# Clamp and integer addition of ten weight blocks on GpSimd, with overlapped steps

## The chip, the cores and the metric

The kernel runs on one core of a Trainium2 chip. The core has five engines, each with its own instruction queue that is worked off strictly in order: TensorE (PE) multiplies matrices into PSUM, VectorE (DVE) and ScalarE (ACT) do elementwise work, GpSimd (POOL) does elementwise work and here also issues the stores of results, and SyncE (SP) issues almost all other transfers (DMA) and computes nothing. Engines wait for each other through semaphores. The metric is the device time of one execution in microseconds, the median of several runs.

## The reference

An attention block without softmax is followed by a token-mixing and a channel-mixing MLP, all in float32:

```python
kv  = einsum('bhsd,bhse->bhde', k, v)             # 8 batches, 8 heads, 576 tokens, 64 per head
out = einsum('bhsd,bhde->bhse', q, kv)
out = out / sqrt(mean(out*out, -1) + 1e-6) * g_norm
x   = out, heads side by side                     # 8 x 576 x 512
u   = x + (relu(x.T @ w_tok1) @ w_tok2).T         # token mixing, 576 -> 256 -> 576
y   = u + relu(u @ w_ch1) @ w_ch2                 # channel mixing, 512 -> 1536 -> 512
```

w_ch1 (512 x 1536) and w_ch2 (1536 x 512) are the channel weights, the subject of the change.

## The kernel before, in words

**Stages.** Batches are worked on in pairs. For each pair the attention makes k'v per head (PSUM tiles ps_kv), multiplies it with q (ps_o, and ps_r for the last 64 tokens), and normalises into tiles x; the token mixing multiplies x with w_tok1 (ps_h), applies ReLU into h, multiplies with w_tok2 and adds x (ps_u), which gives u. POOL stores u (out_dram, and u_rest for the last 64 tokens of each batch). The channel mixing starts at about 183 us and fills the rest, to 768 us. It splits both matrix products into seven smaller ones, two levels deep, with sums of weights and of activations made by DVE. Attention and token mixing of the four pairs, and the preparation of the weights, fill the first 183 us.

**Rounding of weights.** Weights arrive as pairs of 32-bit words and are prepared in blocks by `decode` (L177): ACT scales the raw words (`high` L181 and `low` L186, or L196 and L199 in `scale_leaves` for w_ch2), then DVE does three steps on the block: `clamp` (L202, a minimum and a maximum), `shift` (L206, three bits to the left) and `add` (L211, a custom instruction that adds the other raw word as a 32-bit integer in two 16-bit limbs). There are fourteen channel blocks, numbered 0 to 13 here: eight of w_ch1, 128 partitions x 768 elements, and six of w_ch2, 128 x 1024. `block` (L222) adds `fetch`, the load of the raw words into a tile `raw` (by SP). Four raw tiles exist, so the fetch of block n+4 has to wait until the add of block n has read its tile.

**Order.** It is written out by hand. `start`, `middle`, `steady` and `last` (L1380 onward) are lists of words that `play` (L1319) works through, calling for each word a function that issues instructions; every engine and every DMA queue keeps this program order (`keep`). `kv`, `e`, `a`, `q`, `g`, `t`, `m`, `r`, `i`, `d`, `s`, `p` are steps of the attention of the next pair (`p` is a multiply of x by 1/rms on POOL, L570; `s` the same on ACT, L557; `d` on DVE, L566), `h`, `hr`, `u`, `z` steps of the token mixing, `l`, `lq`, `lr` loads of k, v and q. `f5` is the fetch of channel block 5. A number such as `1` or `2` plays so many steps of `rounding`, the iterator that `stream` (L1306) makes of the channel blocks: 43 steps in all, of which 31 are played in `middle` and `steady` and the others in `last`. The words around the end of the second `steady` list are

```python
"u3 z6 d11 1", "u4 s10 t40 t41 m2 r2 1",
"u5 i2 d20 p21 1", "u6 1 f12 b20 b21", "u7 1", "a3 q30 g31 q31 g30", "u8 t30 t31 m3 r3 f13"]]
```

`x` words transpose finished tiles into the room of w_ch2 that no block has been decoded into yet, and `b` words store these (SP, blocks<-w_ch, L124 like all loads and stores); the decoding of the last blocks has to wait until that room is empty.

**Helpers.** Many operations are recorded at the line of a helper: L124 a DMA on any queue, L127 a sum of two tiles, L130 a ReLU, L133 a copy on ACT, L136 a matrix product.

Of the kernel before, what the change touches and what calls it, by code (L numbers as in the profile page):

```python
# [15 lines left out]
ALU = mybir.AluOpType  # L16
# [4 lines left out]
def kernel(  # L21
# [32 lines left out]
    nc = tc.nc  # L54
    P = 128
    B, S, DM = k.shape
# [7 lines left out]
    NC, NF, NTOK = DM // P, DCH // P, DTOK // P  # L64
# [8 lines left out]
    T = 2 * P  # L73
    assert B // 2 == 4
    EPS = 1e-6
    TOP = (2.0 - 2.0 ** -3 - 2.0 ** -23) * 2.0 ** -96

    def pool(name, bufs, side="left", stack=ctx, **kw):
# [27 lines left out]
    w_ch1 = w1p.tile([P, 4, 4, FQ], F32, name="w_ch1")  # L106
# [8 lines left out]
    def do(f, *a, **kw):  # L115
        return lambda: f(*a, **kw)
# [4 lines left out]
    keep = tc.keep_in_program_order  # L121

    def dma(o, i, engine=nc.sync):
        keep(engine.dma_start(o, i))  # L124
# [49 lines left out]
            q_rest[b] = qtp.tile([P, HP, HF], F32, name="qR", tag="qR", bufs=4)  # L174
            dma(q_rest[b], q[b].rearrange("(c p) s -> p c s", p=P)[..., LO:])

    def decode(dst, raw, flat, leaves=False):  # L177

        bits = dst.bitcast(U32)
        def high():  # L180
            keep(nc.scalar.activation(dst, raw()[..., 1].bitcast(F32), AF.Prelu,  # L181
                                      scale=2.0 ** -112, alpha=2.0 ** 32))

        def low():
            t = raw()[..., 0]
            keep(nc.scalar.activation(t, t, AF.Copy, scale=2.0 ** -29))  # L186

        def scale():
            high()
            low()  # L190

        def scale_leaves():
            of = raw().rearrange("p (g b l j) w -> p g l b j w", g=4, b=NC, l=2)
            to = lambda t, l: t.rearrange("p (g l b j) -> p g l b j", g=4, l=2, b=NC)[:, :, l]
            for l in range(2):
                keep(nc.scalar.activation(to(dst, l), of[:, :, l, ..., 1].bitcast(F32), AF.Prelu,  # L196
                                          scale=2.0 ** -112, alpha=2.0 ** 32))
            for l in range(2):
                keep(nc.scalar.activation(to(raw()[..., 1], l), of[:, :, l, ..., 0], AF.Copy, scale=2.0 ** -29))  # L199

        def clamp():
            keep(nc.vector.tensor_scalar(out=dst, in0=dst, scalar1=TOP, scalar2=-TOP * 2.0 ** 32,  # L202
                                         op0=ALU.min, op1=ALU.max))

        def shift():
            keep(nc.vector.tensor_scalar(out=bits, in0=bits, scalar1=3, scalar2=None,  # L206
                                         op0=ALU.logical_shift_left))

        def add():
            o = bits.bitcast(U16)  # L210
            keep(nc.vector._custom_dve(ADD32_U16LIMBS, out=o, in0=o, in1=flat().bitcast(U16)[..., 2 * leaves:][..., :2]))  # L211

        return scale_leaves if leaves else scale, clamp, shift, add, high, low

    def words(w):
        return w.bitcast(U32).rearrange("r (n w) -> r n w", w=2)
# [2 lines left out]

        return flat if len(dst.shape) == 2 else flat.rearrange("p (a n) -> p a n", a=dst.shape[1])  # L220

    def block(n, loads, dst, leaves=False):  # L222

        raw = []

        def fetch():
            raw.append(stage.tile([P, n, 2], U32, name="raw", tag="raw", bufs=4))
            for o, i in loads(raw[0]):
                dma(o, i)

        def turn():
            t = raw[0]
            return t if len(dst.shape) == 2 else t.rearrange("p (a n) w -> p a n w", a=dst.shape[1])

        return (fetch,) + decode(dst, turn, lambda: raw[0], leaves)

    def get_tok1(i):

        rows = words(moe_w_tok1)[:LO].rearrange("(i j p) n w -> i p j n w", j=2, p=P)
        return block(2 * DTOK, lambda raw: [(raw.rearrange("p (j n) w -> p j n w", j=2), rows[i])], w_tok1[i])  # L240

    def get_tok1_half(j):
        return block(DTOK, lambda raw: [(raw, words(moe_w_tok1)[ts(j, P)])], w_tok1[0][:, j])

    def get_tok1_rem():
        w = words(moe_w_tok1)[LO:]
        return block(DTOK, lambda raw: [(raw[:HF], w), (raw[HF:], w)], w_tok1r)
# [1 line left out]
    def get_tok2(t):  # L249
        return block(S, lambda raw: [(raw, words(moe_w_tok2)[ts(t, P)])], w_tok2[:, t])  # L250

    def get_ch1(c, f):

        return block(2 * FQ, lambda raw: [(raw, words(moe_w_ch1)[ts(c, P), ts(f, 2 * FQ)])],
                     w_ch1[:, 2 * f + c // 2, c % 2:4:2])

    def get_ch2(f):

        def loads(raw):
            t = raw.rearrange("p (f n) w -> p f n w", f=2)  # L260
            rows = words(moe_w_ch2)[ts(f, 2 * P)].rearrange("(f p) n w -> f p n w", f=2)
            return [(t[:, i], rows[i]) for i in range(2)]

        dst = w_ch2[:, 2 * f // NS, ds(2 * f % NS, 2)]
        return block(2 * DM, loads, dst.rearrange("p f h n -> p (f h n)"), True)

# [118 lines left out]
    def attention(pair, groups):  # L387
# [137 lines left out]
        def mean(g):  # L525
            ms = stat[g][0]
            keep(nc.vector.tensor_scalar(out=ms, in0=ms, scalar1=1.0 / D, scalar2=EPS,
                                         op0=ALU.mult, op1=ALU.add))
# [154 lines left out]
    blocks, blocks_dram = {}, {}  # L683
# [621 lines left out]

    def stream(blocks):  # L1306

        def both(f, g):
            return lambda: (f(), g())

        steps = [blocks[0][1]]
        for n in range(len(blocks)):
            clamp, shift, add = blocks[n][2:5]
            if n + 1 < len(blocks):
                shift = both(shift, blocks[n + 1][1])
            steps += [clamp, shift, add]
        return iter(steps)

    def play(lines, after={}, **stages):  # L1319
# [3 lines left out]
        for name in " ".join(lines).split():  # L1323
# [5 lines left out]
            else:  # L1329
# [4 lines left out]
    tok1 = [get_tok1(i) for i in range(J // 2)] + [get_tok1_rem()]  # L1334
    tok2 = [get_tok2(t) for t in range(NTOK)]
    first_rows = [get_tok1_half(j) for j in range(2)]
    channel = ([get_ch1(c, f) for f in range(2) for c in range(NC)]
               + [get_ch2(f) for f in range(NF // 2)])
    dma(g_row, bass.AP(tensor=g_norm.tensor, offset=g_norm.offset, ap=[[0, 1], list(g_norm.ap[0])]), nc.gpsimd)
    load(0)  # L1340
    first_rows[0][0]()
# [32 lines left out]
    def spread_g():  # L1374
# [38 lines left out]
    more |= {f"b{u}{half}": lambda u=u, half=half: put_blocks(u, half, blocks[u, half])  # L1413
             for u in range(3) for half in range(2)}
    rounding = stream(channel)

    def keep_warm(n):
# [23 lines left out]
    for i in range(2):  # L1441
# [4 lines left out]
    last = [  # L1446
        "h00 -i3 -d31 -s30 2 -d40 2 o0", "h01 2 o1", "h10 2 o3", "h11 2 o2", "hr z2 1 o4", "u0 z3 1 c0", "u1 z4 1 c1 o5", "u2 z5 c2",
        "u3 z6 1 c3 o6", "u4 z7 1", "u5 z8 1", "u6 1 s0", "u7 s1 s2", "u8 s3 s4"]
# [100 lines left out]
```

## Time and profile before

| what | us |
|---|---|
| median of three runs (769.94, 769.95, 770.03) | 769.95 |
| span of the profiled execution | 768.2 |
| PE busy in it | 761.7 |
| DVE busy in it | 644.7 |
| POOL busy in it | 112.9 |

The span runs from the first to the last instruction of the profiled execution; the median lies 1.75 us above it. The granted clock of TensorE is 1.00 in all stages.

A group row reads: line, engine, operation, output and inputs by the program's names, shapes and types, number; then busy time in us and mean ns of one; then the idle time of the engine just before them and what ended it. A row of waits reads: engine, tile and line, what it waited for, total us, times, longest. A row of a timeline reads: start in us, duration in us, engine, line, operation, and in brackets the idle time before it with what ended it. For a DMA the time of a row is that of its issue on the queue (SPq, POOL), and not that of the transfer.

### The profile page before, as it was taken

The page shows a single profiled execution, that of the slowest core. Times are in us where ns is not written, and L with a number is a line of the kernel's source. Part 1 is how long each engine was busy: PE and PEld are TensorE (multiplying, and loading weights), DVE is VectorE, ACT ScalarE, POOL GpSimd, SP SyncE. Part 2 cuts the span into 40 slices and gives each one's busy share as a digit, 9 for nine tenths or more (in the row PEclk, how much of TensorE's full clock was granted, in tenths as well). Part 3 has the DMA queues.
Part 4 walks back from the last instruction along what each step waited for, and adds up shares of the span by engine and source line. Part 5 has one row for each costly group of instructions (what it writes and reads, how often), then busy time and mean ns, then how long its engine had stood idle before and what let it go on. Part 6 is the DMA issues. An engine that isn't in the chain of part 4 may idle for free.

```text
span 768.2 us, 12734 instructions
## 1 busy us (share of the span) xinstructions
PE 761.7 (99%) x4694; PEld 613.6 (80%) x4694; DVE 644.7 (84%) x957; ACT 279.8 (36%) x563; POOL 112.9 (15%) x125
## 2 busy tenths in 40 slices
PE   9999999999999999999999999999999999999997
PEld 8655555446888888888888888888888888888887
DVE  4868886997757779899968989997898997798996
ACT  3656666763210232512234241123352223325221
POOL 1003030204410000002240002042000227000204
PEclk9999999999999999999999999999999999999999
DMA  9999997599699785689997578999659889855679
GB/s 353 375 369 372 379 372 271 174 323 345 243 288 322 290 276 175 180 264 215 223 229 248 155 225 214 263 185 266 193 151 296 160 227 209 202 149 159 150 193 120
DMA packets 137966, 188.28 MB, mean 245 GB/s; under 512 B 48689, under 2 KB 95793, under 8 KB 135857
## 3 DMA queue, kind: packets, MB, share of 16 engines
q1 hardware_dynamic: 102096, 168.59, 69.2%
q0 software_dynamic: 34848, 18.36, 16.2%
q8 instruction: 38, 0.62, 0.3%
q10 hardware_dynamic: 960, 0.52, 0.2%
q14 instruction: 24, 0.19, 0.1%
HBM read 138.28 MB, written 49.15 MB: 244 GB/s over the span
## 4 chain that ended last, share of the span: by engine, by line
PE 96%; DMA 2%; DVE 1%; SPq 0%; issue 0%; ACT 0%; DVEq 0%
PE ps_d L136 28%; PE ps_b L136 19%; PE ps_a L136 19%; PE ps_u L136 8%; PE ps_h L136 8%; PE ps_v L136 5%; PE ps_c L136 3%; PE ps_w L136 2%; PE ps_kv L136 2%; PE ps_o L136 2%; DMA raw<-in_moe_w_tok_dram 1%; DMA v_in<-in_k_dram 1%; PE ps_r L136 0%; DVE x L494 0%; DVE ms L522 0%; DVE w_tok L211 0%
## 5 line engine op out<-in xcount | busy, mean ns | idle before, releaser
L136 PE MATMUL ps_d<-ui,w 128*128 128x256 f32 x504 | 118.6, 379 | 0.0
L136 PEld LDWEIGHTS ps_d<-ui,w 128*128 128x128 f32 x504 | 95.8, 190 | 13.0
L133 ACT COPY ps_d<-ps_a 128x768 f32<-128x768 f32 (+1 forms) x56 | 32.0, 572 | 199.9 <-PE ps_a L136 196.9
L127 DVE TENSOR_TENSOR v<-v,v 128x1536 f32<-128x1536 f32 (+2 forms) x70 | 103.2, 1481 | 0.3
L136 PE MATMUL ps_b<-sv,w 128*128 128x256 f32 x324 | 78.9, 379 | 0.0
L136 PE MATMUL ps_a<-v,w 128*128 128x256 f32 x324 | 78.7, 379 | 0.0
L1273 POOL DMA_DIRECT2D out_dram<-us x24 | 26.8, 1834 | 291.8 <-ACT p L133 286.5
L136 PEld LDWEIGHTS ps_b<-sv,w 128*128 128x128 f32 x324 | 61.2, 190 | 8.9 <-issue 0.6
L136 PEld LDWEIGHTS ps_a<-v,w 128*128 128x128 f32 x324 | 61.6, 190 | 8.4
L136 PE MATMUL ps_u<-h,w_tok 128*128 128x512 f32 (+1 forms) x160 | 64.7, 599 | 0.0
L130 ACT ACTIVATE v<-v 128x768 f32<-128x768 f32 (+1 forms) x54 | 42.6, 822 | 55.1 <-DVE v L127 52.3
L136 PE MATMUL ps_d<-v,w 128*128 128x256 f32 x258 | 62.7, 379 | 0.0
L136 PE MATMUL ps_h<-x,w_tok 128*128 128x512 f32 x128 | 57.6, 600 | 0.7 <-DVE w_tok L211 0.6
L1273 POOL DMA_DIRECT2D out_dram<-r x40 | 41.3, 1924 | 102.0 <-ACT p L133 80.3
L136 PE MATMUL ps_d<-sv,w 128*128 128x256 f32 x228 | 55.4, 379 | 0.0
L136 PEld LDWEIGHTS ps_d<-v,w 128*128 128x128 f32 x258 | 48.9, 190 | 6.6
L136 PEld LDWEIGHTS ps_u<-h,w_tok 128*128 128x128 f32 (+1 forms) x160 | 25.6, 179 | 31.1 <-issue 26.7
L136 PEld LDWEIGHTS ps_d<-sv,w 128*128 128x128 f32 x228 | 43.3, 190 | 5.9
L136 PE MATMUL ps_a<-uT,w 128*128 128x256 f32 x192 | 46.7, 379 | 0.0
L136 PEld LDWEIGHTS ps_h<-x,w_tok 128*128 128x128 f32 x128 | 23.5, 190 | 28.4 <-issue 24.2
L136 PE MATMUL ps_b<-ui,w 128*128 128x256 f32 x168 | 40.8, 379 | 0.0
L136 PEld LDWEIGHTS ps_a<-uT,w 128*128 128x128 f32 x192 | 36.5, 190 | 5.0
(178 smaller groups left out, 1296.7 us busy)
## 6 DMA issues: line engine op xcount, KB each, us to landing
w<-parts SPq DMA_DIRECT2D x168, 384.0 KB
w<-parts SPq DMA_DIRECT2D x56, 192.0 KB
uT<-blocks SPq DMA_DIRECT2D x36, 256.0 KB
k_in<-in_k_dram SPq DMA_DIRECT2D x8, 1024.0 KB
v_in<-in_v_dram SPq DMA_DIRECT2D x8, 1024.0 KB
qT<-in_q_dram SPq DMA_DIRECT2D x8, 1024.0 KB
out_dram<-x POOLq DMA_DIRECT2D x16, 512.0 KB, 6.9
raw<-in_moe_w_ch_dram SPq DMA_DIRECT2D x8, 768.0 KB
```

Source lines behind the costliest of these rows:

```text
L127: keep(engine.tensor_tensor(out=o, in0=a, in1=b, op=op))
L130: keep(nc.scalar.activation(o, a, AF.Relu))
L133: keep(nc.scalar.copy(o, a))
L136: keep(nc.tensor.matmul(*a, **kw))
L1273: keep(nc.gpsimd.dma_start(to, t()[ds(b * Q, Q), at].rearrange("p n l j -> p n (l j)"), accum_op=ALU.add))
```

## The change

Blocks 0 to 9 (all eight of w_ch1 and two of w_ch2, `POOLED = 2`) are clamped and added on GpSimd: the clamp as the same two-operation instruction, the addition as a plain 32-bit integer addition of the block and the raw words, which lie 8 bytes apart. The shift stays on DVE, and so do all three steps of blocks 10 to 13. `stream` is re-cut: there are still 43 steps at the same places of the lists. Step 0 scales and clamps block 0. Then come, for each block n, three steps: scaling of block n+1; addition of block n-1 and clamp of block n+1; shift of block n (for the last block, shift and addition). Before, a block had its clamp, its shift (with the scaling of the next block) and its addition one after the other. So an addition comes two steps later than before, and a scaling one step earlier.

```diff
+    POOLED = 2
@@ decode(dst, raw, flat, leaves=False, pooled=False)
         def clamp():
-            keep(nc.vector.tensor_scalar(out=dst, in0=dst, scalar1=TOP, scalar2=-TOP * 2.0 ** 32,
-                                         op0=ALU.min, op1=ALU.max))
+            keep((nc.gpsimd if pooled else nc.vector).tensor_scalar(
+                out=dst, in0=dst, scalar1=TOP, scalar2=-TOP * 2.0 ** 32, op0=ALU.min, op1=ALU.max))
...
         def add():
+            if pooled:
+                keep(nc.gpsimd.tensor_tensor(out=bits, in0=bits, in1=raw()[..., int(leaves)], op=ALU.add))
+                return
             o = bits.bitcast(U16)
             keep(nc.vector._custom_dve(ADD32_U16LIMBS, out=o, in0=o, in1=flat().bitcast(U16)[..., 2 * leaves:][..., :2]))
...
     def stream(blocks):
-        def both(f, g):
-            return lambda: (f(), g())
-        steps = [blocks[0][1]]
-        for n in range(len(blocks)):
-            clamp, shift, add = blocks[n][2:5]
-            if n + 1 < len(blocks):
-                shift = both(shift, blocks[n + 1][1])
-            steps += [clamp, shift, add]
+        last = len(blocks)
+        def part(n, k):
+            if 0 <= n < last:
+                blocks[n][k]()
+        def adds(n):
+            part(n - 1, 4)
+            part(n + 1, 2)
+        def ends():
+            part(last - 1, 3)
+            part(last - 1, 4)
+        steps = [lambda: (part(0, 1), part(0, 2))]
+        for n in range(last):
+            steps += [do(part, n + 1, 1), do(adds, n), do(part, n, 3) if n + 1 < last else ends]
         return iter(steps)
...
-    channel = ([get_ch1(c, f) for f in range(2) for c in range(NC)]
-               + [get_ch2(f) for f in range(NF // 2)])
+    channel = ([get_ch1(c, f, True) for f in range(2) for c in range(NC)]
+               + [get_ch2(f, f < POOLED) for f in range(NF // 2)])
```

The order of PE's instructions is the same as before. On SP, the first load of uT comes ahead of the fetch of block 12, where it came after that of block 13; the other loads and stores keep their order.

More of the change, by code (lines that the diff above doesn't have):

```diff
@@ L175, in load_q_rest, with decode @@
             dma(q_rest[b], q[b].rearrange("(c p) s -> p c s", p=P)[..., LO:])
-    def decode(dst, raw, flat, leaves=False):
+    def decode(dst, raw, flat, leaves=False, pooled=False):
         bits = dst.bitcast(U32)
@@ L220, in like, with block @@
         return flat if len(dst.shape) == 2 else flat.rearrange("p (a n) -> p a n", a=dst.shape[1])
-    def block(n, loads, dst, leaves=False):
+    def block(n, loads, dst, leaves=False, pooled=False):
         raw = []
@@ L233, in turn @@
             return t if len(dst.shape) == 2 else t.rearrange("p (a n) w -> p a n w", a=dst.shape[1])
-        return (fetch,) + decode(dst, turn, lambda: raw[0], leaves)
+        return (fetch,) + decode(dst, turn, lambda: raw[0], leaves, pooled)
     def get_tok1(i):
@@ L250, in get_tok2, with get_ch1, get_ch2 @@
         return block(S, lambda raw: [(raw, words(moe_w_tok2)[ts(t, P)])], w_tok2[:, t])
-    def get_ch1(c, f):
+    def get_ch1(c, f, pooled):
         return block(2 * FQ, lambda raw: [(raw, words(moe_w_ch1)[ts(c, P), ts(f, 2 * FQ)])],
-                     w_ch1[:, 2 * f + c // 2, c % 2:4:2])
-    def get_ch2(f):
+                     w_ch1[:, 2 * f + c // 2, c % 2:4:2], pooled=pooled)
+    def get_ch2(f, pooled):
         def loads(raw):
@@ L264, in get_ch2 @@
         dst = w_ch2[:, 2 * f // NS, ds(2 * f % NS, 2)]
-        return block(2 * DM, loads, dst.rearrange("p f h n -> p (f h n)"), True)
+        return block(2 * DM, loads, dst.rearrange("p f h n -> p (f h n)"), True, pooled)
     SA = {1: 0, 2: 1, 7: 2, 4: 3, 5: 4, 6: 5, 3: 6}
```

## The prediction

> **What bounds the kernel now.** I read the page's busy shares and its chain first, to see which engine has to be kept waiting before time is lost.
>
> ```profile
> PE 761.7 (99%) x4694; PEld 613.6 (80%) x4694; DVE 644.7 (84%) x957; ACT 279.8 (36%) x563; POOL 112.9 (15%) x125
> PE 96%; DMA 2%; DVE 1%; SPq 0%; issue 0%; ACT 0%; DVEq 0%
> ```
>
> TensorE (PE) works for 761.7 of 768.2 us, so only 6.5 us could be won by anything that makes its helpers faster. VectorE (DVE), which the change relieves, is 84% busy but carries 1% of the chain. Next the waits of PE by what ended them:
>
> ```profile
> PE ps_j L136 <- DVE ones L1351: 1.1, 1, 1.1
> PE ps_h L136 <- DVE w_tok L211: 0.6, 1, 0.6
> PE ps_kv L136 <- DMA v_in<-in_v_dram: 0.6, 1, 0.6
> PE ps_d L136 <- DVE xs L127: 0.4, 1, 0.4
> ```
>
> No wait is for a channel weight (w_ch), and in 60 to 185 us, where all fourteen blocks are rounded, the same view is empty. So DVE time saved there buys nothing by itself, and the question becomes which new lateness can reach PE. For that I need durations (groups by shape):
>
> ```profile
> L202 DVE TENSOR_SCALAR w_ch<-w_ch 128x768 f32<-128x768 f32 x8 | 5.2, 646 | 1.1 <-ACT w_ch L181 1.1
> L202 DVE TENSOR_SCALAR w_ch<-w_ch 128x1024 f32<-128x1024 f32 x6 | 4.1, 684 | 0.0
> L211 DVE CUSTOM_DVE_ANT_1 w_ch<-w_ch,raw 128x1536 uint16<-128x1536 uint16 x8 | 7.5, 933 | 0.3
> L211 DVE CUSTOM_DVE_ANT_1 w_ch<-w_ch,raw 128x2048 uint16<-128x2048 uint16 x6 | 8.2, 1365 | 0.3
> L570 POOL TENSOR_TENSOR x<-x,inv 128x512 f32<-128x512 f32 x4 | 5.0, 1246 | 2.5 <-DVE inv L541 2.4
> L127 POOL TENSOR_TENSOR sv<-w_ch,sv 128x384 f32<-128x384 f32 x4 | 4.0, 1002 | 11.2 <-DVE sv L127 11.2
> L1369 POOL MEMSET k_in<- 64x512 f32 x2 | 1.0, 520 | 18.2 <-PE ps_kv L136 18.2
> ```
>
> And the timelines of five engines around one place, about 150 to 167 us, which decides my forecast:
>
> ```profile
> 147.46 1.32 POOL L570 TENSOR_TENSOR x<-x,inv 128x512 f32<-128x512 f32 x1
> 147.78 2.08 DVE L211 CUSTOM_DVE_ANT_1 w_ch<-w_ch,raw 128x2048 uint16<-128x2048 uint16 x1
> 149.93 1.51 SPq L124 DMA_DIRECT2D raw<-in_moe_w_ch_dram  x2
> 151.62 0.76 POOL L124 DMA_DIRECT2D out_dram<-x  x1 [2.83 <-ACT sq L498]
> 151.49 8.64 SPq L124 DMA_DIRECT2D blocks<-w_ch  x8
> 162.70 1.26 ACT L196 ACTIVATE w_ch<-raw 128x512 f32<-128x512 f32 x2 [2.08 <-DMA blocks<-w_ch]
> 163.99 1.25 ACT L199 ACTIVATE raw<-raw 128x512 uint32<-128x512 uint32 x2
> 166.30 0.60 ACT L130 ACTIVATE h<-ps_h 128x512 f32<-128x512 f32 x1 [1.06 <-PE ps_h L136]
> 165.14 1.99 PE L136 MATMUL ps_h<-x,w_tok1r 64*128 64x512 f32 x8
> 167.05 4.13 PE L136 MATMUL ps_u<-h,w_tok 128*128 128x512 f32 x9
> ```
>
> The reader is to see a chain of hand-overs. The add of block 8 on DVE ends at 149.86; 0.07 us later SyncE (SP) may issue the raw fetch of block 12, into the tile that this add has read. Behind it in SP's order stand the eight stores blocks<-w_ch; the last lands at 162.39. ScalarE (ACT) waits for them, because block 12 is decoded into the room that they empty. It scales until 165.24, is idle for 1.06 us, and makes the ReLU h that PE takes at 167.05, only 0.16 us after it ended (166.30 + 0.59 = 166.89).
>
> **The change, part by part.**
>
> *DVE loses* 8 x 0.646 + 2 x 0.684 = 6.5 us of clamps and 8 x 0.933 + 2 x 1.365 = 10.2 us of adds: 16.7 us. What DVE hands to PE between 60 and 165 us is done at least 3 us before PE takes it, so PE gains 0 us.
>
> *GpSimd (POOL) gains* ten clamps and ten adds, which the trace does not show on POOL. The add has two full inputs, so its nearest row is L127 POOL: 1.002 us per 384 elements, that is 2.0 us for 768 and 2.67 for 1024. Low end: the L570 row undisturbed, 1.035 us per 512 (its second input is a small broadcast): 1.55 and 2.07. High end: the slowest L127 POOL, 1.450 us per 384: 2.9 and 3.87. I take 2.0 and 2.67. The clamp moves one stream in and one out. Low end: MEMSET, one stream, 520 ns per 512: 0.78 and 1.04. High end: the two-input price, 2.0 and 2.67. I take 1.0 and 1.3, nearer MEMSET, since no second input has to be fetched. Sum: 8 x 3.0 + 2 x 3.97 = 31.9 us, over about 95 us; by the windows POOL is otherwise busy for 7.0 us of 70 to 112 and 5.2 of 112 to 151. It has room; what matters is its order.
>
> *A stand-still between the two engines.* At 105.98 POOL ran an L570 multiply, and the DVE clamp that began at 106.53 took 1.42 us, against a median of 0.55 for its shape, ending when POOL's did. At 147.46 and 147.78 (above) the same: 2.08 us for an add whose median is 1.22. So a POOL operation holds such DVE operations for about 0.87 us. If each of the twenty does so once, DVE loses 17 us and its relief of 16.7 us is gone; PE's sum is still 0, by the 3 us above. [...]
>
> *The re-cut of the steps*: still 43, but add n is played two steps later (after the next block's shift), and the scaling one earlier. ACT's earlier scaling costs nothing (ACT is 36% busy), except where its tile is late.
>
> *Raw fetches on SP* now wait for adds in POOL's queue, which stand behind POOL's own stores out_dram<-x, each waiting for a DVE sum. First place: the raw fetch of block 6 was issued at 90.28. Its add (block 2) is now behind the stores issued at 95.98 and 101.77, so it ends at about 101.77 + 0.74 + 2.0 = 104.5, and the fetch is 14 us late. Behind it on SP are qT, k_in, v_in and qR of the next pair. They had landed by 109.9, and PE takes qT at 118.91 (landed 100.81, 18 us before) and v_in at 130.08 (landed 109.08, 21 us before). So all 14 us are covered and cost 0; without the cover they would be paid up to 14. The raw tiles of blocks 7 and 8 follow some 9 us later, to about 123 and 126; ACT scales them just before the ReLUs at 128.23, which have 2.9 us until PE takes them: 0.
>
> Second place, the one above. POOL has block 8's add behind the store at 151.62. On DVE the work ahead of that store's sum shrinks: between 147.87 and 150.39 stood an add (2.08) and a clamp (0.68), now a shift (0.69) that POOL's L570 holds to 148.78. The sum starts at about 149.5 rather than 150.39; I count 0.6 us of that, since DVE's earlier steps move too. So the add ends at 151.62 - 0.6 + 0.76 + 2.67 = 154.45 and the fetch goes out at 154.5, 4.6 us late. The eight stores follow at the old distance (12.46 us from the fetch's issue to the last landing), less what they gain because the 0.52 MB of out_dram are now ahead of them: 0.52 MB at the 334 GB/s moved in 151 to 183 us is 1.6 us. So they land 3.0 to 4.6 us late; I take 3.8. ACT's margin is 1.06 + 0.16 = 1.2 us. PE stops for 3.8 - 1.2 = 2.6 us at 167. Ends: add at 2.07 us, full relief (0.9) and full gain (1.6): 2.1 late, 0.9 at PE; add at 3.87, no relief, no gain: 6.4 late, 5.2 at PE. [...]
>
> PE is busy to the end from there, so 2.6 us stay: later work (block 13, the sums that PE takes at 182.9, with 10 us to spare) moves along. Span 768.2 + 2.6 = 770.8; the median of the runs, 769.95, lies 1.75 above the span: 772.5.
>
> **The rivals.** The measurement can tell 0.2%, 1.54 us, from no change.
>
> (a) Absorbed: add at its low end and stores draining faster; the low end above, +0.9, 770.9. For it: the low row is a real POOL row, and the transfer queue is a guess. Against it: the add itself stands behind the store at any price. It decides if the stores land less than 2.7 us late.
>
> (b) POOL dear: clamps at 2.0 and 2.67 us, adds at 2.9 and 3.87. Then 167 costs 5.2, and PE is also reached through ACT's x scaling (L557, after DVE's inv), which has 1.04 us to spare at 79.71 and 1.28 at 159.47: a shift on DVE that waits for a clamp 1 us longer and a held operation of 0.87 exceed that by some 0.8 us at each of about three places: 5.2 + 2.4 = +7.6, 777.5. For it: no POOL operation on 768 strided words is in the trace. Against: the width rows.
>
> (c) Faster: DVE's 16.7 us reach PE after all. Place: PE's 6.5 us of idleness. Price: its named DVE waits are 1.1 and 0.6 before 28 us, outside the change, and 0.4 late; to be faster than 0.2% all 0.4 and 1.1 us of unnamed pauses would have to go. 768.2.
>
> **How the numbers follow.** Main case 0.55 (771.5 to 775.5), (b) 0.16 (775.5 up), (a) 0.23 (769.7 to 771.5), (c) 0.06. The range 769.7 to 780 leaves out (c) and the far half of (b). Faster 0.06; same 0.23; slower 0.71.
>
> **What would show it.** Right: PE's waits gain one line of 2 to 3 us, ps_u on ACT h, near 167; POOL's busy time grows by about 32 us, DVE's falls by less than 16.7; SP's queue waits for POOL w_ch. Wrong: POOL clamps above 2 us, a PE wait before 165, or blocks<-w_ch landing as early as before.

## The result, and the profile after

The changed kernel takes 774.31 us (median of six runs, 771.70 to 775.44) against 770.03 us before (six runs, 769.94 to 770.50): ratio 1.005, 95% interval 1.0035 to 1.0065. It is slower. The forecast was 772.5. Two of the six runs lie at 771.7 and 772.3 us, where TensorE's mean granted clock was 1.000; the other four, 773.5 to 775.4, had 0.997. The profiled run is the one of 772.34 us, span 770.5.

The lines that answer to those shown of before, first the page's busy shares and chain, then the waits of PE:

```profile
PE 762.1 (99%) x4694; PEld 613.9 (80%) x4694; DVE 640.2 (83%) x937; ACT 279.2 (36%) x563; POOL 141.6 (18%) x145
PE 87%; DMA 6%; DVE 2%; ACT 2%; SPq 1%; issue 1%; POOL 0%; ACTq 0%; POOLq 0%; DVEq 0%
```

```profile
PE ps_u L137 <- ACT h L131: 2.1, 1, 2.1
PE ps_j L137 <- DVE ones L1363: 1.1, 1, 1.1
PE ps_h L137 <- DVE w_tok L215: 0.6, 1, 0.6
PE ps_d L137 <- DVE xs L128: 0.4, 1, 0.4
PE ps_kv L137 <- DMA v_in<-in_v_dram: 0.3, 1, 0.3
```

One wait is new, 2.1 us, and it is the one forecast: PE for ACT's h. The span grew by 770.5 - 768.2 = 2.3 us. PE's share of the chain fell from 96% to 87% because the chain, followed back from this wait, now leaves PE for the transfers and for ACT. The durations of the moved work (groups by shape, 60 to 185 us):

```profile
L212 POOL TENSOR_TENSOR w_ch<-w_ch,raw 128x768 uint32<-128x768 uint32 x8 | 15.1, 1894 | 4.4 <-DVE w_ch L207 4.3
L203 POOL TENSOR_SCALAR w_ch<-w_ch 128x768 f32<-128x768 f32 x8 | 7.0, 881 | 10.4 <-ACT w_ch L182 10.4
L212 POOL TENSOR_TENSOR w_ch<-w_ch,raw 128x1024 uint32<-128x1024 uint32 x2 | 5.2, 2598 | 1.1 <-DVE w_ch L207 1.1
L203 POOL TENSOR_SCALAR w_ch<-w_ch 128x1024 f32<-128x1024 f32 x2 | 2.1, 1056 | 0.0
```

The chain of hand-overs, from the timelines of POOL, SP, ACT and PE:

```profile
152.35 0.76 POOL L125 DMA_DIRECT2D out_dram<-x  x1 [1.70 <-issue]
153.12 2.42 POOL L212 TENSOR_TENSOR w_ch<-w_ch,raw 128x1024 uint32<-128x1024 uint32 x1
155.56 0.81 SPq L125 DMA_DIRECT2D raw<-in_moe_w_ch_dram  x2
156.47 6.51 SPq L125 DMA_DIRECT2D blocks<-w_ch  x8
166.16 1.25 ACT L197 ACTIVATE w_ch<-raw 128x512 f32<-128x512 f32 x2 [4.80 <-DMA blocks<-w_ch]
168.63 2.04 ACT L131 ACTIVATE h<-ps_h 128x512 f32<-128x512 f32 x4
169.26 3.27 PE L137 MATMUL ps_u<-h,w_tok 128*128 128x512 f32 x7 [2.08 <-ACT h L131]
```

The reader is to see each step of the forecast in it. POOL's add of block 8 stands behind the store, and SP's fetch goes out 0.02 us after the add ends (155.54). Then come the eight stores; ACT, which had waited 2.08 us for them, waits 4.80; and the ReLU, which had started at 166.30 after 1.06 us of idleness, starts at 168.63 with none.

### The profile page after: what moved, and what is told of

It is laid out like the page before. It is cut to its first block, busy times and chain, and to the rows that moved or that the text cites. A ratio compares the mean times of both kernels' runs of the same rounds, so it can differ in the third digit from the quotient of the medians.

```text
span 770.5 us, 12738 instructions
## 1 busy us (share of the span) xinstructions
PE 762.1 (99%) x4694; PEld 613.9 (80%) x4694; DVE 640.2 (83%) x937; ACT 279.2 (36%) x563; POOL 141.6 (18%) x145
## 4 chain that ended last, share of the span: by engine, by line
PE 87%; DMA 6%; DVE 2%; ACT 2%; SPq 1%; issue 1%; POOL 0%; ACTq 0%; POOLq 0%; DVEq 0%
PE ps_d L137 28%; PE ps_b L137 19%; PE ps_a L137 19%; PE ps_u L137 6%; PE ps_v L137 5%; PE ps_h L137 4%; PE ps_c L137 3%; PE ps_w L137 2%; DMA raw<-in_moe_w_ch_dram 2%; DMA raw<-in_moe_w_tok_dram 1%; DMA k_in<-in_k_dram 1%; PE ps_kv L137 1%; PE ps_o L137 1%; DMA v_in<-in_k_dram 1%; SPq L125 1%
```

## The experiments

Each was run beside the kernel before on the same chip; e1 to e8 ran on one chip, e9 on a second, e10 and e11 on a third. Ratios are to the kernel before.

**e1: the stores ahead of the fetch.** The changed kernel with one word moved:

```diff
-        "u5 i2 d20 p21 1", "u6 1 f12 b20 b21", "u7 1", ...
+        "u5 i2 d20 p21 1", "u6 1 b20 b21 f12", "u7 1", ...
```

> Theory (one place: block 12's fetch waits on SP for POOL's add of block 8, and the eight stores blocks<-w_ch stand behind it): with the stores in front of the fetch, ACT's scaling no longer waits 4.8 us for them, PE's wait for ACT h (2.1 us) is gone, and the time is that of the kernel before, 769.9 to 770.4 us, at clock 1.000 in every run. Rival (the 29 us of POOL work or its hold on DVE cost time elsewhere): it stays above 771.5. Rival for the slower runs of the changed kernel (clock 0.997, 773.5 to 775.4): if POOL work lowers the clock, 0.997 appears here too; if PE's stand-still does, it does not.

Measured: 771.06 us (11 runs, 770.17 to 771.82), 1.001 (1.0001 to 1.0018), clock 0.999 to 1.000 in every run. The wait of PE on ACT h is gone from the profile (a run of 770.37 us, span 768.5):

```profile
PE ps_j L137 <- DVE ones L1363: 1.1, 1, 1.1
PE ps_h L137 <- DVE w_tok L215: 0.6, 1, 0.6
PE ps_d L137 <- DVE xs L128: 0.4, 1, 0.4
PE ps_kv L137 <- DMA v_in<-in_v_dram: 0.2, 1, 0.2
```

So the main place is shown: with all twenty POOL operations where they were, moving eight stores past one fetch takes the 2.1 us away. But the time was forecast at 769.9 to 770.4, and eight of eleven runs lie near 771. Something smaller is left.

**e2: the re-cut steps alone, all on DVE.**

```diff
-    channel = ([get_ch1(c, f, True) ... [get_ch2(f, f < POOLED) ...
+    channel = ([get_ch1(c, f, False) ... [get_ch2(f, False) ...
```

> The re-cut steps alone, with clamps and adds all on DVE. Theory: the add of block 8 comes right after the sum that the out_dram store waits for, at about 150.1 us, costs 1.22 us there and not 2.4 behind a store on POOL; the fetch of block 12 is about 1.5 us late, little more than ACT's margin of 1.2: PE waits 0 to 0.3 us, 769.9 to 770.3 us. Rival (the later add of the re-cut is enough for the loss, wherever it runs): PE waits 2 us and more, above 771.5.

Measured: 771.32 us (770.21 to 772.49), 1.0015 (1.0006 to 1.0024). The profile, of a run of 770.21 us, has no new wait of PE: ACT's scaling of block 12 starts at 163.97, 1.3 us later than the 162.70 of before, about as much as the margin of 1.2. The forecast of 769.9 to 770.3 was missed: the median lies 1.2 us above the kernel before, against 4.3 for the changed kernel. The later adds of the re-cut thus do a part of the harm without POOL, though less than the whole; where the slower runs lost their time, this profile does not show.

**e3: POOL's clamps and adds in the steps of before.** `stream` is that of the kernel before:

```diff
-        steps = [lambda: (part(0, 1), part(0, 2))]
-        for n in range(last):
-            steps += [do(part, n + 1, 1), do(adds, n), do(part, n, 3) if n + 1 < last else ends]
+        steps = [blocks[0][1]]
+        for n in range(len(blocks)):
+            clamp, shift, add = blocks[n][2:5]
+            if n + 1 < len(blocks):
+                shift = both(shift, blocks[n + 1][1])
+            steps += [clamp, shift, add]
```

> POOL clamps and adds, in the steps of the kernel before. Theory: the add of block 8 now stands ahead of the out_dram store at 152 us, ends at about 151.4 and lets the fetch go 1.5 us late; PE waits at 167 for 0 to 0.4 us, 769.9 to 771 us, unless DVE's shifts, which then follow a POOL clamp at once, run late elsewhere. Rival (POOL's work itself is the loss): above 771.5. If both halves are needed, e2 and e3 are near 770 and only their combination is slow.

Measured: 772.50 us (772.30 to 774.08), 1.0036 (1.0022 to 1.0049). The forecast of 769.9 to 771 was missed. The fetch of block 12 did go out early (151.63), and PE did not wait for h. It waited elsewhere; from the waits of PE and the timelines of POOL, DVE and PE:

```profile
PE ps_h L137 <- ACT x L561: 2.1, 1, 2.1
149.20 2.41 POOL L212 TENSOR_TENSOR w_ch<-w_ch,raw 128x1024 uint32<-128x1024 uint32 x1
151.59 1.03 POOL L203 TENSOR_SCALAR w_ch<-w_ch 128x1024 f32<-128x1024 f32 x1
152.66 0.69 DVE L207 TENSOR_SCALAR w_ch<-w_ch 128x1024 uint32<-128x1024 uint32 x1 [3.61 <-POOL w_ch L203]
157.11 2.41 POOL L212 TENSOR_TENSOR w_ch<-w_ch,raw 128x1024 uint32<-128x1024 uint32 x1
157.13 2.43 DVE L541 SCALAR_TENSOR_TENSOR ms<-ms,inv 128x16 f32<-128x16 f32 x1
```

First a shift on DVE waits 3.6 us for POOL's clamp of block 9, which stands behind the add of block 8; then a tiny operation of the normalisation (16 elements per partition, 0.17 us at this place in the profile of before) takes 2.43 us and ends with the POOL add of 2.41 us that began beside it. ACT's scaling of x follows them, and PE stands still from 160.05 to 162.16. This is the route of rival (b), at a price of the clamp (1.03 us) at which the prediction had not opened it: the clamp was late by its place in POOL's queue, not by its price, and the hold was 2.3 us (2.43 - 0.17), not 0.87. What the re-cut buys is that DVE need not wait for POOL; what it costs is late adds.

**e4: the add of block 8 alone back on DVE.**

```diff
-            if pooled:
+            if pooled and add_too:
...
-        return block(2 * DM, loads, dst.rearrange("p f h n -> p (f h n)"), True, pooled)
+        return block(2 * DM, loads, dst.rearrange("p f h n -> p (f h n)"), True, pooled, f > 0)
```

> As the changed kernel, but the add of block 8 alone goes back to DVE. Theory: it no longer stands behind POOL's store, takes 1.2 us instead of 2.4, and the fetch of block 12 goes out about 2.5 us earlier than the 155.56 of the changed kernel; PE's wait falls from 2.1 to 0 to 0.6 us: 769.9 to 770.7 us. Rival (the other nineteen POOL operations are the loss): above 771.5.

Measured: 771.63 us (770.16 to 772.04), 1.0017 (1.0008 to 1.0026); two runs at 770.2 and 770.4, nine near 771.6, so the median lies 0.9 us above the forecast. One add out of twenty takes back more than half of the loss and, as in e1, all of the wait on h. The profile is of a run of 771.59 us, and here the remainder is seen:

```profile
PE ps_h L137 <- ACT x L561: 1.0, 1, 1.0
126.19 0.89 ACT L182 ACTIVATE w_ch<-raw 128x768 f32<-128x768 f32 x1 [7.76 <-DMA raw<-in_moe_w_ch_dram]
152.88 1.21 DVE L215 CUSTOM_DVE_ANT_1 w_ch<-w_ch,raw 128x2048 uint16<-128x2048 uint16 x1
159.24 2.02 ACT L561 ACTIVATE x<-x,inv 128x64 f32<-128x64 f32 x8 [1.03 <-DVE inv L545]
161.31 5.42 PE L137 MATMUL ps_h<-x,w_tok 128*128 128x512 f32 x12 [0.98 <-ACT x L561]
```

ACT stood at the scaling of block 7, which starts, when its raw tile has landed, 1.2 us later than in the changed kernel's profile (125.01); up to about 152 us the steps of DVE, ACT and POOL are 1.2 us late with it. Before, that scaling started at 122.18 without a wait. But the late tile is only half of it, as the profile of e1 shows, where the tile was as late:

```profile
126.11 0.90 ACT L182 ACTIVATE w_ch<-raw 128x768 f32<-128x768 f32 x1 [7.70 <-DMA raw<-in_moe_w_ch_dram]
157.98 2.02 ACT L561 ACTIVATE x<-x,inv 128x64 f32<-128x64 f32 x8 [1.03 <-DVE inv L545]
```

There ACT scaled x at 157.98, and no wait of PE is listed. In e4 it scaled x 1.26 us later still, because the add of block 8, back on DVE, takes 1.21 us in front of the normalisation. So the 1.0 us of e4 needs both, the late tile and the edit of e4 itself.

**e5 and e6: the first place mended, alone and with the second.** e5 moves the fetch of block 6 (raw tiles in the order of SP) behind the loads of the next pair; e6 has this and the edit of e1:

```diff
-        ... "hr z2 f5 f6", "a1 q10 g11 q11 g10 lq0", "kv10 kv11 e10 e11 t10 t11 m0 r0", "u0 i0 1",
-        "u1 z4 d00 s01 l1", "u2", ...
+        ... "hr z2 f5", "a1 q10 g11 q11 g10 lq0", "kv10 kv11 e10 e11 t10 t11 m0 r0", "u0 i0 1",
+        "u1 z4 d00 s01 l1 f6", "u2", ...
```

> As the changed kernel, but the fetch of block 6 stands behind the loads of k, v and the main part of q on SP, so these no longer wait 14 us with it. Theory (two late places: the raw tile of block 7, for which ACT waits 6.6 us before 126 us and which makes the rest up to 167 us late by a varying amount, and the stores behind block 12's fetch): ACT's waits on DMA raw (7.8 us) fall below 2, the spread of the runs falls under 1 us, but the stores are still late: PE waits 0.5 to 2.1 us on ACT h, 770.5 to 772.3 us. Rival (the first place costs nothing): no change against the changed kernel, 771.7 to 775.4.

> Both places mended: fetch of block 6 behind the loads, stores ahead of the fetch of block 12. All POOL work stays. Theory: PE's waits are those of the kernel before, all runs within 0.4 us, 769.9 to 770.3 us; DVE's 16.7 us still buy nothing. Rival (POOL's work or its hold on DVE costs time in itself): above 770.8, with a wait of PE on ACT x or DVE.

Measured: e5 772.56 us (771.58 to 773.92), 1.0032 (1.0021 to 1.0044); PE's wait on h is 1.6 us, ACT's waits on raw tiles fell from 7.8 to 3.1 us, not below 2, and the spread did not fall under 1 us: two runs of six had a clock of 0.997, and the four at 1.000 lie between 771.58 and 773.09. The median missed its forecast by 0.3 us. e6 770.05 us (11 runs, 769.92 to 770.29), 0.9998 (0.9989 to 1.0006). Busy shares, waits of PE and one timeline row of e6:

```profile
PE 762.3 (99%) x4694; PEld 614.6 (80%) x4694; DVE 640.1 (83%) x937; ACT 279.5 (36%) x563; POOL 141.5 (18%) x145
PE ps_j L137 <- DVE ones L1363: 1.1, 1, 1.1
PE ps_h L137 <- DVE w_tok L215: 0.6, 1, 0.6
PE ps_d L137 <- DVE xs L128: 0.4, 1, 0.4
118.90 0.94 ACT L182 ACTIVATE w_ch<-raw 128x768 f32<-128x768 f32 x1
```

POOL's twenty operations are all there (141.5 us busy), DVE's relief too, and the time is that of the kernel before. So in this order of the steps the work on POOL costs nothing in itself, and the relief buys nothing. All of the loss goes when two places of one queue are mended; e1, which lacks only the first of them, took 771.06 us on the same chip, so there the first place was worth about 1.0 us.

**e7 and e8: a stand-still without POOL.** To see where the runs at clock 0.997 come from, the kernel before was given four (e7) or eight (e8) repeats of one ReLU:

```diff
                 for t in range(NTOK):
-                    relu(h1[side][:, t], acc[side, t])
+                    for _ in range(5 if pair == B // 2 - 1 and side == t == 0 else 1):   # e8: 9
+                        relu(h1[side][:, t], acc[side, t])
```

> The kernel before, with the first ReLU of the last pair done four times more on ACT (same values), which makes PE stand still at 167 us by about 4 x 0.52 - 0.16 = 1.9 us and changes nothing else. Theory (a stand-still costs its own length): 771.9 us. Rival (a stand-still of this size also lowers the clock for a while, as the runs of the changed kernel at clock 0.997 suggest): some runs at 0.997 and 773.5 to 775.

> The same with eight more ReLUs: PE stands still for about 8 x 0.52 - 0.16 = 4.0 us. Theory: 774.0 us at clock 1.000. Rival (clock): 0.997 or lower in most runs and about 2 us on top, 776.

Measured: e7 four runs at 772.39 to 772.81 us (clock 0.999) and one at 774.65 (0.997), which is the profiled one; e8 four runs at 776.50 to 779.17, clock 0.995 to 0.997; ratios 1.0036 (1.0023 to 1.0048) and 1.0107 (1.0091 to 1.0122). In the profiled runs (774.65 and 776.50) the stand-stills were 2.3 and 4.8 us, more than the 1.9 and 4.0 forecast (a repeat took 0.57 us, not 0.52, in e7). The windows of PE in e7, with columns stretch, length, PE busy (instructions), granted clock, DMA share and GB/s:

```profile
164.00:168.00 4.00, 3.47 (x12) 1.00 1.06 326
168.00:172.00 4.00, 2.19 (x3) 0.79 1.04 357
172.00:176.00 4.00, 4.00 (x9) 0.78 1.02 371
176.00:180.00 4.00, 4.00 (x11) 1.00 1.02 370
```

After the wait the clock averages 0.79 and 0.78 over two stretches and is then back. PE's 40 products ps_u take 17.57 us there, and 17.57 in the profile of e8, where the stretch 172 to 176 has 0.57. So the theory that a stand-still costs its own length failed in all runs of e8 and in one of e7. The three runs of e8 at 0.995 took another 1.5 to 2.7 us; no profile shows where.

**e9: the changed kernel again**, for a profile of a run at 0.997.

> The changed kernel unaltered, beside the same runs of the kernel before as e5 to e8 had on this chip. Theory (a stand-still of 2 us or more at 167 us, made longer in some runs by the late raw tile of block 7, and in some of them followed by some 8 us at a lower clock): runs fall in two groups, about 771.7 to 772.5 at clock 0.999 to 1.000 and 773.5 to 775.5 at 0.997; where the profile shows 0.997, the loss of clock lies within 10 us after PE's wait on ACT h and nowhere else. Rival (the clock is lowered by something that POOL's work does): the lower clock lies elsewhere, or begins before the wait.

Measured: 773.51 us (six runs), 1.0045 (1.0028 to 1.0063): three runs at 772.41 to 772.49 (clock 0.999) and three at 774.5 to 776.7 (0.995 to 0.997). Of the profiled run, 774.53 us, the products ps_u and the windows of 1 us behind the wait, with the columns of e7:

```profile
169.99 17.56 PE L137 MATMUL ps_u<-h,w_tok 128*128 128x512 f32 x40 [2.20 <-ACT h L131]
170.00:171.00 1.00, 1.00 (x2) 0.80 1.20 312
171.00:172.00 1.00, 1.00 (x2) 0.50 1.08 375
172.00:173.00 1.00, 1.00 (x3) 0.50 1.08 399
173.00:174.00 1.00, 1.00 (x3) 0.50 1.07 396
174.00:175.00 1.00, 1.00 (x4) 0.99 1.06 393
```

The shorter windows show what the 4 us stretches of e7 average over: the clock falls to one half, 0.50, and comes back. What the five windows lack to full clock sums to 1.7 us, which is about 3.4 us at half clock (an estimate from these rows); the same windows of e7 (0.67, 0.50, 0.50, 0.63 from 170 to 174) and e8 (0.64, 0.50, 0.50, 0.66 from 172 to 176) lack 1.7 us in sum too. In the first profile of the changed kernel, with a stand-still of 2.08 us and full clock, the same 40 products took 15.87 us. So the lower clock costs 17.56 - 15.87 = 1.7 us; the spans differ by 772.8 - 770.5 = 2.3 us, and the other 0.6 is that PE reached the wait later (167.79 against 167.18).

In the profile of e9 the lower clock comes after the wait and not elsewhere between 100 and 760 us (1.00 in the windows up to 168 us and from 176 us on); e7 has it (0.50) without any added POOL work, while e6 has all POOL work and no run below 0.999. So in these runs the lower clock goes with the stand-still and not with POOL's work. Its length alone does not decide: four runs of e7 kept the clock (0.999) and took 2.3 to 2.7 us more than the kernel before, which is the stand-still of 2.3 us itself. What does decide between runs of the same kernel is not shown.

**e10 and e11: e1 and e2 once more**, for profiles of their slower runs.

> The kernel of e1 once more, for a profile of one of its runs near 771.1 us (its first profile showed one of 770.4, in which PE did not wait). Theory: the late raw tile of block 7 (first place) reaches PE at 161 us, a wait on ACT x of 0.7 to 1.0 us, as in the profile of e4. Rival: the 0.9 us lie elsewhere, as many small waits of PE or a lower clock.

> The kernel of e2 once more, for the same reason: its runs lay between 770.2 and 772.5 us, its profile showed one of 770.2. Theory: with the re-cut steps alone the raw tile of block 7 is late too (ACT waited 5.8 us for it), and a run of 771 us and more has a wait of PE on ACT x near 161, or on ACT h near 167, of its size. Rival: no such wait, and the time is spread.

Measured: e10 770.14 us (eight runs, one of them above 770.6), 1.0003 (0.9992 to 1.0014); e11 770.55 us, 1.0005 (0.9993 to 1.0016), so on this chip neither loss is clear, and the kernel before has a run of 771.21 there too. Neither profile shows a new wait of PE; in both ACT still waits for the raw tile of block 7 (6.8 and 5.9 us), which in e10 came at 125.02, 1.1 us earlier than in the profile of e1. So on this chip that lateness did not reach PE. What the slower runs of e1 and e2 lost was not caught in a profile. A wait like that of e4 at 161 us is a possible form of it, but in e1 it would need a tile later than the 126.11 that was seen; that is argued, not shown.

## Why the prediction was right, point by point

**Sign, size and place.** Slower, by one new wait of PE on ACT h near 167, for the reason given: right, and shown by e1 and e4. The wait was 2.08 us against 2.6, and the profiled span grew by 2.3 against 2.6.

**The term that was missing.** "PE is busy to the end from there, so 2.6 us stay" is the step that failed. Behind such a stand-still the granted clock fell to 0.50 in the profiled runs of e7 and e9, for about 3.4 us (estimated above from the 1 us windows of e9); the 40 products ps_u took 17.56 us in e9 instead of 15.87, so 1.7 us more. The mean clock of these two runs was 0.997, and that of four of the six runs of the changed kernel too. With it the median, 774.31, lies 1.8 above the forecast although the profiled wait was shorter than forecast: the two runs at full clock lie at 771.7 and 772.3, below the forecast, and the four at 0.997 above. None of these four was profiled, and three of them lie 2.8 to 3.1 us above the profiled run, so 1.7 us do not account for all of it. The fall stands in the profiles behind waits of 2.20 us (e9), 2.34 us (e7) and 4.85 us (e8), and is not in those with a wait of 1.6 us (e5) and 2.08 us (the first of the changed kernel), where every window is at 1.00. From what length of a wait on it comes is not shown.

**POOL's prices.** Clamps 0.88 and 1.06 us (taken 1.0 and 1.3), adds 1.89 and 2.60 (taken 2.0 and 2.67), 29.4 us together against 31.9. The rows chosen, L127's linear price for two full inputs and one near MEMSET's for the clamp, were good. Seven of the eight adds of 768 took about 1.86. The 2.42 us for the add of block 8 lies below the 2.67 taken, the 2.78 us for that of block 9 above it.

**The fetch of block 12** went out 5.6 us late, not 4.6. The add was cheaper by 0.25, but "I count 0.6 us of that" for DVE's relief was wrong in sign: the store that the add stands behind came 0.73 us later than before (152.35 against 151.62). DVE had been held in front of that sum; rows of DVE and POOL of the changed kernel:

```profile
144.48 2.95 DVE L531 TENSOR_SCALAR ms<-ms 128x24 f32<-128x24 f32 x1
144.51 1.86 POOL L212 TENSOR_TENSOR w_ch<-w_ch,raw 128x768 uint32<-128x768 uint32 x1
146.33 1.06 POOL L203 TENSOR_SCALAR w_ch<-w_ch 128x1024 f32<-128x1024 f32 x1
149.65 1.55 DVE L207 TENSOR_SCALAR w_ch<-w_ch 128x1024 uint32<-128x1024 uint32 x1
```

An operation that took 0.18 us in the profile of before (mean of its three) took 2.95 us here, through an add and the clamp after it. The prediction had 0.87 us a hold.

**The stores** landed 3.5 us late by ACT's start (166.16 against 162.70), 3.8 taken: the transfers gave back 5.6 - 3.5 = 2.1 us, more than the 0.8 that was the middle of the estimate; why they gave back so much is open. The two errors nearly cancelled, and that the wait came out so near the forecast is in so far luck. **ACT's margin** of 1.2 us held: 3.46 - 1.2 = 2.3 against a PE start 2.21 us later (169.26 against 167.05).

**DVE's relief** was worth nothing to PE: right (e6). DVE's busy time fell by 4.5 us and not by 16.7, so 12.2 us went into being held: between 60 and 185 us operations that the change left on DVE took longer by about that much (L531 on 24 elements 5.9 us instead of 0.5, the shifts 11.0 instead of 8.9, L570 10.4 instead of 8.2, and smaller ones). "A POOL operation holds such DVE operations" was right, its size too small at single places (2.95 - 0.18 = 2.77 us against 0.87) and too large in sum (17).

**The first place**, "all 14 us are covered and cost 0": the loads of q, k and v were covered, and so were the ReLUs h, 1.9 us late at 130.11. The raw tile of block 7 was not quite: its scaling started at 125.01 (tile reckoned: "about 123"), after ACT had stood still for 6.6 us, and later steps follow it: in e1, where it started 1.1 us later, ACT's scaling of x did too (157.98 against 156.86). In e5, with this place mended, the wait at 167 was 1.6 instead of 2.1 us; e6 against e1 shows about 1.0 us on one chip, and e10 none on another. So it was worth between 0 and 1 us, where 0 was put. How it reached PE with the second place mended is not shown, and the edit of e5 also brings the loads forward; no profile has PE waiting for a load after 60 us.

**The rivals.** (c), faster, and (a), absorbed, did not happen. (b)'s prices did not come, but its route did, in e3.

## What to carry to other kernels

Before moving a step to an engine with room, look at what else that engine's queue holds: here an add behind a store made the fetch that waits for the add depend on the store's own wait (it went out at 155.56 instead of 149.93 us), and this single fetch at the head of the loading queue held back eight stores that had nothing to wait for (from 156.47 us on; with the order changed in e1, from 148.41). The busy shares (POOL 15%, DVE 84%) said nothing of this; the margin of the one hand-over (0.16 us at PE, 1.06 at ACT) and the order in the queue said all of it, and moving two words of the order gave the loss back, though none of the versions tried is faster than the kernel before. And where the matrix engine is the bound, as here, look at what follows a new stand-still of it too: the stand-stills of 2.2 and 2.3 us in e9 and e7 cost another 1.7 us in the profiled runs.

## What the runs showed of the hardware that had not been expected

- A stand-still of TensorE of 2.2 to 2.3 us was followed in two profiled runs (e7, e9) by a granted clock of 0.50, for about 3.4 us (an estimate from the 1 us windows), which cost 1.7 us over the 40 products that follow. The mean clock of both runs was 0.997. Mean clocks of 0.997 or less came in one of five runs of e7, three of six of e9, four of six of the first runs of the changed kernel, one of five of e3 (stand-still 2.1 us in its profile) and two of six of e5 (1.6 us); after 4.8 us, in all four runs.
- A DVE operation on 24 elements per partition, 0.18 us in the profile of before, took 2.95 us beside two POOL operations that followed each other (add and clamp, 144.51 to 147.39): it ended at 147.43, with the second and not between them. The group of these three operations went from a mean of 178 to 1951 ns.
- Plain integer addition of 32-bit words on GpSimd, with one input 8 bytes apart, took in most cases 1.85 us for 768 elements per partition, and 2.42 and 2.78 for 1024; a clamp with two operations took in most cases 0.83 us for 768, and 1.06 for 1024.
